# A static TensorE schedule: instruction blocks counted by true phase and size, and one output group split in two

## The chip, the cores and the metric

The program runs on one core of a Trainium2 chip. The metric is the device time in microseconds of one launch; of the kernel before there are three runs and one execution under the profiler. Engines are named as in the profile: PE (matmul; PEld is its weight load), DVE, ACT, POOL and SP (which only issues DMAs here).

## What is computed

A linear-attention recurrence over 768 steps (4 x 8 heads, state 40 x 40), whose output feeds two dense layers over 3072 tokens of width 320:

```
y[t]  = r[t] . state
Sa    = state . a[t]
state = state * w[t] - Sa (x) b[t] + v[t] (x) k[t]
x1 = gelu_like(x0 @ w_in) @ w_out            # d_ff 2048, h * sigmoid(1.702 h)
out = (silu(x1 @ w_gate) * (x1 @ w_val)) @ w_out2   # d_ff 1536
```

All inputs are float32. The small products of the recurrence are float32 matmuls; the wide ones split each operand into two float32r parts.

## The kernel before

**Three stages.** The recurrence is done in 12 steps of 64 tokens. Each step is some twenty small groups of matmuls (`Attention.prepare` builds a step's triangular inverse, `Attention.advance` its output and the next state), joined by work on DVE and ACT. The first dense layer (`Up`) needs the output of two steps for each of its six token blocks; its *wide parts* are 16 `h_part` (8 matmuls of 512 columns, L479) and 16 `o_part` (8 matmuls, L506 to L513) for each block, 192 in all. Recurrence and first layer are interleaved on PE by a planner; this is the stage up to some 739 us. The second layer (`Down`, L1392 and L1411 to L1413) follows, in an order of its own that the change does not touch. While the last wide parts run (the *tail* of the plan, after the last step's output), each `h_part` also sets off eleven small jobs that load and split `Down`'s weights.

**The planner.** `Plan.add` takes a task with its engine, a guessed cost, what it reads and writes, and a due time (for a step's groups its number, for wide parts 1e6: whenever nothing else is due). `Plan.order` simulates all engines and puts the tasks into one order, which the program then follows engine by engine without any choice at run time. So costs and rules of the planner set nothing but order, and how many *fillers* PE gets: `warm` (L437) is a matmul on zeros into a bank that nobody reads, put where PE would idle and its clock could fall.

**Instruction blocks in the planner.** The planner assumes that PE's instructions come in blocks of `BLOCK` = 256, and that a block takes `FETCH` = 3.8 us to come. `count` guesses a task's instructions from its cost, `cross` adds a stall where a task ends a block before the next is there, and two rules act on it: if a small group would run into a block's end too early, a wide part is taken first (`PACE`, `AHEAD`), and if none is ready, fillers bridge the gap (`BRIDGE`). A float32 matmul as written is two weight loads and two matmuls, so that a group of 32 is 128 instructions; a wide part is 16, a filler 2.

```
        c = t.choice["PE"]
        return 16 if t.due >= 1e6 or c < 1.05 else 128 if c < 1.7 else 256 if c < 3 else 384
```

The guess starts the count at 0 and takes 256 for the state update `m_one` of steps 1 to 4, which is 34 matmuls of two kinds and a drain.

**The output group.** In `advance`, `y_one` (L1115) multiplies the old state with r (`y_state` twice with a drain between, L1096) and then adds the part of the own tokens (`y_part`, L1110): one task of 64 matmuls on PE, cost 2.5. `y_mm` adds the last part, `y_out` on DVE scales the sum, `give` hands it to the dense layer.

**Accumulators of the first layer.** At the end of a token block the three accumulators in `sums` are drained by ACT L529, DVE L532, ACT L539 and DVE L541; the next block's first `o_part` (L511) waits for L541.

Of the kernel before, what the change touches and what calls it, by code (L numbers as in the profile page):

```python
# [51 lines left out]
class Task:  # L52
    def __init__(self, n, eng, cost, fn, deps, due, bank, kb, same, port):
        self.n, self.fn, self.due, self.deps, self.bank, self.kb, self.same = n, fn, due, deps, bank, kb, same
        self.port = port
        self.choice = dict(zip(eng, cost)) if isinstance(eng, tuple) else {eng: cost}
        self.pick = isinstance(eng, tuple)
        self.heirs, self.left, self.est = [], len(deps), {}
        self.eng = self.begin = self.end = None
# [12 lines left out]
class Plan:  # L72
# [4 lines left out]
    WINDOW, KEEP, DENSITY, WIDE, STILL = 3.4, 4000.0, 1600.0, 5000.0, 640.0  # L77
    BLOCK, FETCH, PACE, AHEAD = 256, 3.8, 0.5, 0.5
    BRIDGE = True
# [7 lines left out]

    def add(self, eng, cost, fn, reads=(), writes=(), due=0.0, after=(), bank=None, kb=0, into=(), same=None, port=True, work=None):
        deps = {d for d in after if d}
# [9 lines left out]
        t = Task(len(self.tasks), eng, cost, fn, deps, due, bank, kb, same, port)  # L99
        t.work = work  # L100
        for d in deps:
# [10 lines left out]
    def count(self, t):  # L112

        c = t.choice["PE"]
        return 16 if t.due >= 1e6 or c < 1.05 else 128 if c < 1.7 else 256 if c < 3 else 384

# [6 lines left out]
    def order(self):  # L123

        free, ready, done = {"PE": self.START}, {}, []
        sets = [0.0] * self.sets
        wire = port = hold = began = 0.0
        sent, pe = 0, []

# [23 lines left out]

        def cross(k, now, cost):
            nonlocal sent, began
            stop, left = 0.0, self.BLOCK - sent % self.BLOCK
            if k >= left:
                x = now + cost * left / k
                stop = max(0.0, began + self.FETCH - x)
                began = x + stop  # L160
            sent += k
            return stop

        def filler(t, now):
            w = self.fill(t, now)
            w.end += cross(2, now, w.end - now)
            done.append(w)
            pe.append((w.begin, w.end, self.STILL))
            return w.end
# [4 lines left out]
        while True:  # L174
# [8 lines left out]
            if e == "PE":  # L183
                k, size = self.count(t), self.BLOCK
                if t.due < 1e6 and (sent % size + k) / size * self.FETCH > now + t.choice[e] - began + self.PACE:
                    wide = [x for x in found if x[1] == 1e6 and x[0] <= now + self.AHEAD]
                    if wide:
                        now, _, _, e, t = wide[0]
                        k = self.count(t)
            for o in t.choice:  # L190
                ready[o].remove(t)
            if e == "PE":
# [4 lines left out]
                if t.due < 1e6 and hold < 1e8:  # L197
# [8 lines left out]
                    if self.BRIDGE:  # L206
                        left = size - sent % size
                        if k >= left:
                            x = began + self.FETCH - now - t.choice[e] * left / k
                            for _ in range(int(x / self.JUNK)):  # L210
                                now = filler(t, now)
                stop = cross(k, now, t.choice[e])
                pe.append((now, now + t.choice[e] + stop, load))
# [343 lines left out]
class Attention:  # L557
# [79 lines left out]
    def prepare(self, plan, n, due):  # L637
# [89 lines left out]

        plan.add("PE", 2.4, nb_mm, (ak, "kb1"), ("nb.p",), due + 0.15, bank=b, into=(nbk,), work=1760)
        plan.add(("ACT",), (1.05,), nb_out, ("nb.p",), (nbk,), due + 0.16, bank=b)
# [40 lines left out]
        def pieces():  # L770
# [89 lines left out]

            plan.add("PE", 2.7, cross_mm, ("xa", "dd"), ("x.p",), due + 0.1, bank=bx, into=("q0", "q1"), work=2900)
            plan.add(("ACT",), (0.62,), lambda e: move(e, bx, self.q), ("x.p",), ("q0", "q1"), due + 0.1, bank=bx)
            plan.add("PE", 2.3, join_mm, ("tn", "q0", "q1"), ("tt.p",), due + 0.1, bank=bt, into=("tt0", "tt1"), work=1280)
            plan.add(("ACT",), (0.62,), lambda e: move(e, bt, tt[:, :, 32:64]), ("tt.p",), ("tt0", "tt1"), due + 0.1,
# [87 lines left out]
    def advance(self, plan, n, due):  # L952
# [33 lines left out]
        if n:  # L986
            seen = plan.add("PE", 1.2, w_two, (ak, "mt"), ("w.p",), due, bank=bw)
        plan.add(("ACT",), (0.74,), w_out, ("w.p",), ("w",), due, bank=bw)
# [81 lines left out]
        if n + 1 < NT:  # L1070
            plan.add("PE", 2.6 if 0 < n < self.EARLY else 1.25, m_one, ("v", "tok0", "mt"), ("m.p",), due + 0.005, bank=bm,
                     work=4300 if 0 < n < self.EARLY else 2200, after=(middle,))
            plan.add("PE", 1.25, m_two, ("u", "tok1"), ("m.p",), due + 0.02, bank=bm, work=2200)
# [27 lines left out]
        def y_part(j, x):  # L1101
            ps = self.ps[by.slot]
            l = self.tok[j].rearrange("q i e -> q (i e)")
            for k in range(8):
                for r in range(2):
                    for p in range(2):
# [6 lines left out]
                        )  # L1113

        def y_one():  # L1115
            if n:
                y_state(1)
                nc.tensor.drain()
                y_state(0)
            y_part(0, self.sv)  # L1120
# [4 lines left out]
        def y_out():  # L1125
# [3 lines left out]

        plan.add("PE", 2.5 if n else 1.25, y_one, ("md", "r", "tok0", "sv"), ("y.p",), due + 0.045, bank=by,  # L1130
                 work=4300 if n else 2500, after=(marks,))
        plan.add("PE", 1.25, y_mm, ("tok1", "su"), ("y.p",), due + 0.05, bank=by, into=("su",),
# [645 lines left out]
```

## Time and profile before

| | us |
|---|---|
| median of 3 runs | 1143.59 |
| lowest and highest | 1138.55, 1144.63 |
| the profiled execution | 1140.57 |
| its span, first to last instruction | 1138.8 |
| PE busy | 1094.7 (96%) |
| DVE busy | 698.1 (61%) |
| ACT busy | 438.1 (38%) |
| POOL busy | 108.8 (10%) |

The span is the stretch that the profiler sees; the profiled execution's own time is 1.8 us longer. A matmul's end is modelled, so that "busy" hides short gaps between matmuls; idle time before an instruction is told apart by what ended it, and "issue" is a wait that ended with no semaphore: PE's sequencer had nothing to hand over.

### The profile page before, as it was taken

The numbers are of one execution on the slowest core, as the hardware profiler recorded it, in microseconds if no ns is written. First come the engines' busy times: TensorE is split into PE (matmuls) and PEld (weight loads), VectorE is DVE, ScalarE is ACT, GpSimd is POOL, SyncE is SP. The second block draws the span as 40 slices with busy tenths as digits, with TensorE's granted clock in tenths as the row PEclk, the third lists the DMA queues.
The fourth block names the chain that finished last, engine by engine and source line by source line (L and its number), as shares of the span: only waits on it lengthen the run. The fifth ranks groups of instructions, "written<-read, shape, count | busy, mean of one in ns | idle before, by whom it ended". The sixth has DMA issues, their size and how long they took to land.

```text
span 1138.8 us, 39991 instructions
## 1 busy us (share of the span) xinstructions
PE 1094.7 (96%) x17403; PEld 908.4 (80%) x17403; DVE 698.1 (61%) x1461; ACT 438.1 (38%) x809; POOL 108.8 (10%) x124
## 2 busy tenths in 40 slices
PE   9888999989999899999999989999999999999987
PEld 7667777767788777877788768788888888888877
DVE  7875788855968687787966166676344344434321
ACT  2434466543434343434335355545222222222221
POOL 1111223301010000000000022221000000000000
PEclk9898999999999999999899999999999999999999
DMA  7245457552534343443423265744233434343000
GB/s 217 88 154 166 149 165 226 159 177 73 180 103 151 112 137 117 134 150 91 145 64 112 83 204 161 218 122 111 75 106 99 129 103 144 93 127 91 24 1 27
DMA packets 141018, 141.99 MB, mean 125 GB/s; under 512 B 16032, under 2 KB 131744, under 8 KB 140832
## 3 DMA queue, kind: packets, MB, share of 16 engines
q1 hardware_dynamic: 134784, 131.48, 38.6%
q10 hardware_dynamic: 6048, 7.86, 2.1%
q8 instruction: 138, 2.26, 0.8%
q14 instruction: 48, 0.39, 0.1%
HBM read 118.04 MB, written 13.11 MB: 115 GB/s over the span
## 4 chain that ended last, share of the span: by engine, by line
PE 84%; DVE 6%; issue 3%; DMA 3%; SPq 2%; ACT 1%; POOL 0%; ACTq 0%; DVEq 0%; POOLq 0%
PE gv L1392 23%; PE h L479 13%; PE sums L511 4%; PE h L437 4%; PE oacc L1413 4%; PE oacc L1412 4%; PE oacc L1411 4%; PE sums L512 3%; PE sums L513 3%; PE ps L1110 2%; PE ps L1034 2%; PE ps L1160 2%; PE sums L507 2%; PE sums L506 2%; PE ps L885 1%
## 5 line engine op out<-in xcount | busy, mean ns | idle before, releaser
L1392 PE MATMUL gv<-xst,wg 128*128 128x512 f32 x1152 | 274.7, 391 | 0.0
L1392 PEld LDWEIGHTS gv<-xst,wg 128*128 128x128 f32 x1152 | 213.8, 188 | 41.3
L479 PE MATMUL h<-xst,wi 120*128 120x512 f32 x768 | 201.8, 405 | 0.4 <-ACT sg L487 0.3
L479 PEld LDWEIGHTS h<-xst,wi 120*128 120x128 f32 x768 | 142.0, 191 | 33.4 <-ACT sg L487 1.6
L1397 DVE TENSOR_TENSOR sg<-gv,sg 128x512 f32<-128x512 f32 x72 | 49.8, 691 | 169.9 <-PE gv L1392 169.2
L487 ACT ACTIVATE sg<-h 128x512 f32<-128x512 f32 x96 | 57.2, 596 | 174.7 <-PE h L479 162.9
L494 DVE TENSOR_TENSOR gl<-sg,gh 128x512 fp32r<-128x512 f32 x82 | 57.5, 701 | 81.7 <-ACT gh L493 81.7
L1398 ACT ACTIVATE gh<-sg 128x512 fp32r<-128x512 f32 x72 | 45.5, 632 | 137.1 <-DVE sg L1397 137.1
L307 POOL TENSOR_TENSOR cvw<-cvu,cva 128x256 uint32<-128x256 uint32 (+2 forms) x89 | 70.9, 798 | 251.1 <-DVE cvu L299 117.9
L1396 ACT ACTIVATE sg<-gv 128x512 f32<-128x512 f32 x72 | 42.9, 596 | 129.1 <-PE gv L1392 128.4
L1413 PE MATMUL oacc<-wo,gl 128*128 128x320 f32 x288 | 89.6, 311 | 0.0
L1412 PE MATMUL oacc<-wo,gh 128*128 128x320 f32 x288 | 89.4, 310 | 0.0
L1411 PE MATMUL oacc<-wo,gh 128*128 128x320 f32 x288 | 89.2, 310 | 0.0
L511 PE MATMUL sums<-gh,wo 128*128 128x512 f32 x192 | 82.0, 427 | 5.8 <-DVE sg L541 4.6
L1399 DVE TENSOR_TENSOR gl<-sg,gh 128x512 fp32r<-128x512 f32 x72 | 49.8, 692 | 50.3 <-ACT gh L1398 50.3
L512 PE MATMUL sums<-gh,wo 128*128 128x512 f32 x192 | 76.5, 399 | 0.0
L513 PE MATMUL sums<-gl,wo 128*128 128x512 f32 x192 | 76.1, 396 | 0.0
L437 PE MATMUL h<-still 128*128 128x512 f32 x232 | 71.4, 456 | 2.0 <-DVE still L396 1.2
L752 DVE TENSOR_TENSOR tsol<-tsol,tmp 128x126 f32<-128x126 f32 (+22 forms) x217 | 58.3, 269 | 6.7
L493 ACT ACTIVATE gh<-sg 128x512 fp32r<-128x512 f32 x96 | 60.7, 632 | 3.5
L744 DVE TENSOR_TENSOR tmp<-tsol,nsol 128x126 f32<-128x126 f32 (+22 forms) x217 | 56.9, 262 | 6.7
L437 PEld LDWEIGHTS h<-still 128*128 128x128 f32 x232 | 47.8, 217 | 12.9 <-DVE still L396 1.2
(176 smaller groups left out, 1652.9 us busy)
## 6 DMA issues: line engine op xcount, KB each, us to landing
wo<-w_out SPq DMA_DIRECT2D x192, 160.0 KB
cva<-out SPq DMA_DIRECT2D x128, 128.0 KB
cva<-gv SPq DMA_DIRECT2D x96, 128.0 KB
kb<-kba SPq DMA_DIRECT2D x92, 104.0 KB
cva<-in_ab SPq DMA_DIRECT2D x64, 120.0 KB
r<-rT SPq DMA_DIRECT2D x48, 104.0 KB
vt<-vT SPq DMA_DIRECT2D x48, 104.0 KB
a<-kba SPq DMA_DIRECT2D x46, 104.0 KB
```

The costliest lines, as they stand in the source:

```text
L307: nc.gpsimd.tensor_tensor(w.bitcast(U32), u, lo, op=ALU.add)
L437: self.nc.tensor.matmul(self.ph[0].rearrange("q (k c) -> q k c", k=4), c, c.unsqueeze(1).to_broadcast([128, 4, 128]), start=True, stop=True)
L479: nc.tensor.matmul(ps[:, 0:n], self.wi[:, b, 128 * f:128 * f + 128], x[:, a], start=(e == 0), stop=(e == 7))
L493: add("ACT", 0.63, lambda: nc.scalar.activation(out=hi, in_=sg, func=ACTF.Copy), (f"sg{s}",), (f"gh{d}",))
L511: nc.tensor.matmul(acc[k], w[:, c:c + 128], hi, start=st, stop=False)
L512: nc.tensor.matmul(acc[k], w[:, 256 + c:384 + c], hi, start=False, stop=False)
L513: nc.tensor.matmul(acc[k], w[:, c:c + 128], lo, start=False, stop=sp)
L752: self.engine(e).tensor_tensor(t, t, self.tmp[:, 0:(16 - o) * u].rearrange("q (c i) -> q c i", c=16 - o), op=ALU.add)
L1392: nc.tensor.matmul(ps, w[:, b], x[:, a], start=(i == 0), stop=(i == 7))
L1411: nc.tensor.matmul(acc[k], hi[:, c], self.wo[:, f, 0], start=st, stop=False)
L1412: nc.tensor.matmul(acc[k], hi[:, c], self.wo[:, f, 1], start=False, stop=False)
L1413: nc.tensor.matmul(acc[k], lo[:, c], self.wo[:, f, 0], start=False, stop=sp)
```

## The change

Four things change in the planner and in how tasks are declared to it. The count of instructions starts at 63 instead of 0 (`HEAD`), and tasks may give their true `size`. Each task gets a second duration, `least` (`real`), which is what the trace shows of it when nothing stops it, beside its guessed cost; the time that PE has worked in the block (`lean`) is added up from these. A block is now taken to need `FETCH` = 3.4 us, against a mean (`SURE` = 0.5) of that work and the planned time since the block began; `cross` may pass several block ends in one task. And `y_one` is cut in two tasks, `y_old` with both `y_state` (129 instructions) and `y_one` with `y_part`, between which other work may stand. No arithmetic is changed.

```
-    BLOCK, FETCH, PACE, AHEAD = 256, 3.8, 0.5, 0.5
+    BLOCK, FETCH, PACE, AHEAD, HEAD, SURE = 256, 3.4, 0.5, 0.5, 63, 0.5
...
     def count(self, t):
-        c = t.choice["PE"]
-        return 16 if t.due >= 1e6 or c < 1.05 else 128 if c < 1.7 else 256 if c < 3 else 384
+        return t.size or (16 if t.due >= 1e6 or t.choice["PE"] < 1.05 else 128)
+
+    def least(self, t):
+        c = t.choice["PE"]
+        return t.real or (1.87 if t.due >= 1e6 else min(c, 1.15))
...
-        sent, pe = 0, []
+        sent, pe = self.HEAD, []
...
-        def cross(k, now, cost):
-            nonlocal sent, began
-            stop, left = 0.0, self.BLOCK - sent % self.BLOCK
-            if k >= left:
-                x = now + cost * left / k
-                stop = max(0.0, began + self.FETCH - x)
-                began = x + stop
-            sent += k
+        def spare(x, y):
+            return began + self.FETCH - x if self.SURE >= 1.0 else self.FETCH - y - self.SURE * max(0.0, x - began - y)
+
+        def cross(k, now, cost, real):
+            nonlocal sent, began, lean
+            stop, part = 0.0, k
+            left = self.BLOCK - sent % self.BLOCK
+            while part >= left:
+                x = now + stop + cost * (k - part + left) / k
+                y = lean + real * left / k
+                stay = max(0.0, spare(x, y))
+                stop += stay
+                began, lean = x + stay, 0.0
+                sent, part, left = sent + left, part - left, self.BLOCK
+            sent += part
+            lean += real * part / k
             return stop
...
-                if t.due < 1e6 and (sent % size + k) / size * self.FETCH > now + t.choice[e] - began + self.PACE:
+                if t.due < 1e6 and (sent % size + k) / size * self.FETCH - self.PACE > self.FETCH - spare(
+                    now + t.choice[e], lean + self.least(t)
+                ):
...
-            plan.add("PE", 2.6 if 0 < n < self.EARLY else 1.25, m_one, ("v", "tok0", "mt"), ("m.p",), due + 0.005, bank=bm,
-                     work=4300 if 0 < n < self.EARLY else 2200, after=(middle,))
+            plan.add("PE", 2.6 if 0 < n < self.EARLY else 1.25, m_one, ("v", "tok0", "mt"), ("m.p",), due + 0.005, bank=bm,
+                     work=4300 if 0 < n < self.EARLY else 2200, after=(middle,),
+                     size=137 if 0 < n < self.EARLY else 128, real=2.5 if 0 < n < self.EARLY else 1.1)
...
+        def y_old():
+            y_state(1)
+            nc.tensor.drain()
+            y_state(0)
+
         def y_one():
-            if n:
-                y_state(1)
-                nc.tensor.drain()
-                y_state(0)
             y_part(0, self.sv)
...
-        plan.add("PE", 2.5 if n else 1.25, y_one, ("md", "r", "tok0", "sv"), ("y.p",), due + 0.045, bank=by,
-                 work=4300 if n else 2500, after=(marks,))
+        if n:
+            plan.add("PE", 1.25, y_old, ("md", "r"), ("y.p",), due + 0.045, bank=by, work=2200, after=(marks,), size=129)
+        plan.add("PE", 1.25, y_one, ("tok0", "sv"), ("y.p",), due + 0.045, bank=by, work=2100, after=(marks,))
```

Other tasks get `size=` or `real=` in the same way: `nb_mm` 256 and 1.44, `cross_mm` 261 and 2.5, `join_mm` 256 and 1.28, `w_two` 129.

In the built program PE has 220 fillers instead of 232; 48 instead of 40 wide parts stand in the tail. Line numbers of the change are 16 to 22 higher.

**First place: PE, the output of step 6** (L1160, in the change L1182, makes the scores; L1096, now L1116, is `y_state`; L1110, now L1130, is `y_part`; L479, now L495, is an `h_part`). Before:

```order
L1160 MATMUL ps_122<-r,ut 64x64 x32
L1096 MATMUL ps_123<-r,md 64x64 x2
L1096 MATMUL ps_123<-r,md 40x64 x2
...
L1110 MATMUL ps_123<-sv,tok_136 64x64 x2
L1110 MATMUL ps_123<-sv,tok_136 40x64 x2
...
L479 MATMUL h<-xst_93,wi 128x512 x8
```

and in the change:

```order
L1116 MATMUL ps_123<-r,md 64x64 x2
L1116 MATMUL ps_123<-r,md 40x64 x2
...
L495 MATMUL h<-xst_94,wi 128x512 x8
L1130 MATMUL ps_123<-sv,tok_136 64x64 x2
L1130 MATMUL ps_123<-sv,tok_136 40x64 x2
```

An `h_part` now stands between the two halves of the group; before, 96 small matmuls as written followed each other without a wide part.

**Second place: PE, the inverse of step 3** (L842 and L848, now L859 and L865, are `cross_mm`; L941, now L960, are the two token transposes; L511 is the first row of an `o_part`; L856, now L873, is `join_mm`). Before:

```order
L479 MATMUL h<-xst_93,wi 128x512 x8
L842 MATMUL ps_123<-cst 128x512
L848 MATMUL ps_123<-nsol,tsol 16x32 x64
L941 MATMUL ps_122<-cst,kb 128x104 x8
L511 MATMUL sums<-gh_99,wo_106 128x512
...
L856 MATMUL ps_123<-q,tn 32x32 x64
L437 MATMUL h<-still 128x512 x3
L941 MATMUL ps_122<-cst,kb 128x104 x8
L1160 MATMUL ps_123<-r,vt 64x64 x32
```

and in the change:

```order
L495 MATMUL h<-xst_93,wi 128x512 x8
L859 MATMUL ps_122<-cst 128x512
L865 MATMUL ps_123<-nsol,tsol 16x32 x64
L960 MATMUL ps_123<-cst,kb 128x104 x8
L960 MATMUL ps_122<-cst,kb 128x104 x8
L527 MATMUL sums<-gh_100,wo_105 128x512
...
L873 MATMUL ps_122<-q,tn 32x32 x64
L495 MATMUL h<-xst_93,wi 128x512 x8
L1182 MATMUL ps_122<-r,vt 64x64 x32
```

The second transpose moved ahead of the `o_part`, and an `h_part` stands in place of the three fillers behind `join_mm`.

**Third place: ACT, the accumulators of the fifth token block, in the tail** (L291, now L307, begins the work on a loaded weight piece `cva`; L1305, now L1327, rounds one; L529, now L545, drains the first accumulator). Before:

```order
L493 ACTIVATE gh_99<-sg_96 128x512
L291 ACTIVATE cva_76<-cva_76 128x256
L1305 ACTIVATE wo_10893<-cvw_79 128x256
L291 ACTIVATE cva_77<-cva_77 128x256
L529 ACTIVATE sg_98<-sums 128x512
```

and in the change:

```order
L509 ACTIVATE gh_99<-sg_96 128x512
L307 ACTIVATE cva_76<-cva_76 128x256
L1327 ACTIVATE wg<-cvw_79 64x2x128 x2
L545 ACTIVATE sg_98<-sums 128x512
```

One weight piece fewer stands between the rounding of `gh` and the first accumulator, since the tail's jobs begin four `h_part` earlier.

## Rows read from the trace of the kernel before

**Rows 1.** Page, head and part 1: span, busy time by engine.

```profile
span 1138.8 us, 39991 instructions
PE 1094.7 (96%) x17403; PEld 908.4 (80%) x17403; DVE 698.1 (61%) x1461; ACT 438.1 (38%) x809; POOL 108.8 (10%) x124
```

**Rows 2.** Windows by stage: length, busy of each engine (instructions), PE clock, DMA.

```profile
121.00:644.00 523.00, 503.69 (x12146) 405.82 (x12137) 380.36 (x821) 227.50 (x399) 54.40 (x51) 0.98 0.44 134
644.00:739.00 95.00, 90.59 (x379) 72.48 (x380) 57.94 (x126) 51.93 (x115) 23.32 (x30) 0.96 0.65 191
739.00:1138.80 399.80, 390.71 (x2016) 343.53 (x2014) 167.61 (x320) 113.44 (x208) 11.94 (x16) 0.99 0.30 89
```

**Rows 3.** Waits of PE: line, what it waited for, total, times, longest.

```profile
PE sums L511 <- DVE sg L541: 4.6, 2, 4.0
PE ps L941 <- issue: 4.5, 2, 3.0
...
PE ps L1096 <- DVE su L1166: 0.5, 1, 0.5
...
PE ps L996 <- issue: 0.2, 1, 0.2
```

**Rows 4.** DMA queues: the one that carries instructions (packets, MB, share).

```profile
q8 instruction: 138, 2.26, 0.8%
```

**Rows 5.** Timeline of PE, output of step 6: start, length, shape, count [idle before].

```profile
379.83 1.18 PE L1160 MATMUL ps<-r,ut 40*64 40x64 f32 x64
380.81 1.45 PE L1096 MATMUL ps<-r,md 40*64 40x64 f32 x64
382.07 0.53 PE L1110 MATMUL ps<-sv,tok 64*40 64x64 f32 x19
384.99 0.87 PE L1110 MATMUL ps<-sv,tok 64*64 64x64 f32 x45 [2.40 <-issue]
385.79 3.58 PE L479 MATMUL h<-xst,wi 120*128 120x512 f32 x8
```

**Rows 6.** Timeline of PE, the inverse of step 3.

```profile
181.06 0.39 PE L511 MATMUL sums<-gh,wo 128*128 128x512 f32 x1
...
182.08 1.25 PE L856 MATMUL ps<-q,tn 32*32 32x32 f32 x124
184.22 0.25 PE L856 MATMUL ps<-q,tn 32*32 32x32 f32 x4 [0.89 <-issue]
```

**Rows 7.** Timeline of PE, `nb_mm` of step 8 and the wait behind it.

```profile
431.49 1.44 PE L720 MATMUL ps<-kb,a 40*32 40x32 f32 x128
434.10 0.40 PE L511 MATMUL sums<-gh,wo 128*128 128x512 f32 x1 [1.17 <-issue]
```

**Rows 8.** Timeline of PE in step 9: small groups and an `o_part` without a wait.

```profile
522.95 1.14 PE L996 MATMUL ps<-w,tt 64*64 64x40 f32 x64
523.90 1.11 PE L1034 MATMUL ps<-v,tok 64*64 64x40 f32 x64
524.95 0.50 PE L511 MATMUL sums<-gh,wo 128*128 128x512 f32 x1
...
526.99 1.06 PE L1034 MATMUL ps<-u,tok 64*64 64x40 f32 x61
```

**Rows 9.** Timeline of PE: 43 fillers in a row.

```profile
20.75 10.04 PE L437 MATMUL h<-still 128*128 128x512 f32 x43
```

**Rows 10.** Chain that ended last, tail, fifth block's accumulators: start, us, what.

```profile
668.11 1.85 PE h L479 x8
...
674.49 3.75 DMA cva<-gv
...
678.66 0.58 ACT sg L529
...
681.36 0.80 PE sums L511
```

**Rows 11.** Windows: as rows 2, two stretches behind a wait.

```profile
386.00:389.50 3.50, 3.50 (x16) 2.27 (x19) 0.77 (x4) 0.09 (x1) 0.00 (x0) 0.51 0.16 53
679.60:686.40 6.80, 5.04 (x12) 3.98 (x13) 3.03 (x7) 2.87 (x6) 1.18 (x2) 0.50 0.74 241
```

**Rows 12.** Timeline of PE, step 10: a small group that waited for DVE.

```profile
562.68 1.34 PE L885 MATMUL ps<-tt,nb 32*32 32x32 f32 x64 [1.46 <-DVE nk L927]
563.95 1.95 PE L965 MATMUL ps<-v,nk 64*64 64x40 f32 x64
```

More of the change, by code (lines that the diff above doesn't have):

```diff
@@ L55, in __init__ @@
         self.port = port
+        self.work = self.size = self.real = None
         self.choice = dict(zip(eng, cost)) if isinstance(eng, tuple) else {eng: cost}
@@ L86, in __init__, with add @@
         self.sets = sets
-    def add(self, eng, cost, fn, reads=(), writes=(), due=0.0, after=(), bank=None, kb=0, into=(), same=None, port=True, work=None):
+    def add(self, eng, cost, fn, reads=(), writes=(), due=0.0, after=(), bank=None, kb=0, into=(), same=None, port=True, work=None,
+            size=None, real=None):
         deps = {d for d in after if d}
@@ L99, in add @@
         t = Task(len(self.tasks), eng, cost, fn, deps, due, bank, kb, same, port)
-        t.work = work
+        t.work, t.size, t.real = work, size, real
         for d in deps:
@@ L126, in order @@
         sets = [0.0] * self.sets
-        wire = port = hold = began = 0.0
-        sent, pe = 0, []
+        wire = port = hold = began = lean = 0.0
+        sent, pe = self.HEAD, []
         def offer(t):
@@ L165, in filler @@
             w = self.fill(t, now)
-            w.end += cross(2, now, w.end - now)
+            w.end += cross(2, now, w.end - now, 0.23)
             done.append(w)
@@ L208, in order @@
                         if k >= left:
-                            x = began + self.FETCH - now - t.choice[e] * left / k
+                            x = spare(now + t.choice[e] * left / k, lean + self.least(t) * left / k)
                             for _ in range(int(x / self.JUNK)):
                                 now = filler(t, now)
-                stop = cross(k, now, t.choice[e])
+                stop = cross(k, now, t.choice[e], self.least(t))
                 pe.append((now, now + t.choice[e] + stop, load))
@@ L726, in nb_out @@
             self.copy(e, self.flat(nb), self.ps[b.slot].rearrange("q r x -> q (r x)"), -1.0)
-        plan.add("PE", 2.4, nb_mm, (ak, "kb1"), ("nb.p",), due + 0.15, bank=b, into=(nbk,), work=1760)
+        plan.add("PE", 2.4, nb_mm, (ak, "kb1"), ("nb.p",), due + 0.15, bank=b, into=(nbk,), work=1760,
+                 size=256, real=1.44)
         plan.add(("ACT",), (1.05,), nb_out, ("nb.p",), (nbk,), due + 0.16, bank=b)
@@ L859, in move @@
                 self.copy(e, dst, self.ps[b.slot][:, 0].rearrange("q (i t) -> q i t", t=32))
-            plan.add("PE", 2.7, cross_mm, ("xa", "dd"), ("x.p",), due + 0.1, bank=bx, into=("q0", "q1"), work=2900)
+            plan.add("PE", 2.7, cross_mm, ("xa", "dd"), ("x.p",), due + 0.1, bank=bx, into=("q0", "q1"), work=2900,
+                     size=261, real=2.5)
             plan.add(("ACT",), (0.62,), lambda e: move(e, bx, self.q), ("x.p",), ("q0", "q1"), due + 0.1, bank=bx)
-            plan.add("PE", 2.3, join_mm, ("tn", "q0", "q1"), ("tt.p",), due + 0.1, bank=bt, into=("tt0", "tt1"), work=1280)
+            plan.add("PE", 2.3, join_mm, ("tn", "q0", "q1"), ("tt.p",), due + 0.1, bank=bt, into=("tt0", "tt1"), work=1280,
+                     size=256, real=1.28)
             plan.add(("ACT",), (0.62,), lambda e: move(e, bt, tt[:, :, 32:64]), ("tt.p",), ("tt0", "tt1"), due + 0.1,
@@ L986, in advance @@
         if n:
-            seen = plan.add("PE", 1.2, w_two, (ak, "mt"), ("w.p",), due, bank=bw)
+            seen = plan.add("PE", 1.2, w_two, (ak, "mt"), ("w.p",), due, bank=bw, size=129)
         plan.add(("ACT",), (0.74,), w_out, ("w.p",), ("w",), due, bank=bw)
```

## Prediction

> **What bounds the kernel now.** I read the page's head first: PE is busy in 96% of the span [rows 1], so only what stands on PE itself can shorten it. Next the windows by stage: the second layer, 739 to 1138.8 us, keeps PE busy in 391 of 400 us [rows 2], and the change does not touch it. What the change can move lies in the first 739 us, above all in the steps from 121 to 644 us, where PE is busy 504 of 523 us at a mean clock of 0.98, and in the tail behind them [rows 2].
>
> Then the waits of PE. Eleven of its rows end with "issue", from 4.5 us down to 0.2 us, and sum to 18.6 us [rows 3]; no semaphore ended them. The timeline shows what they are. In the output of step 6 PE stops for 2.40 us in the midst of one group, after 19 of its 64 matmuls [rows 5]; in `join_mm` of step 3 it stops 0.89 us after 124 of 128 [rows 6]. Nothing inside a group waits for another engine. Counting PE's instructions in the built program (two weight loads and two matmuls for each float32 matmul as written, drains and semaphore waits too), these two stops stand within two places of 72 x 256 + 193 and 35 x 256 + 193, and the one behind `nb_mm` [rows 7] of 80 x 256 + 193. So they recur by blocks of 256. The queue of kind "instruction" carried 138 packets of 16.4 KB each [rows 4], while PE ran 34,806 matmuls and weight loads [rows 1], 252 for each packet. I take it from this that PE stops where the next block of 256 has not come, and that the block ends lie at 193 behind a multiple of 256, that is, 63 places off a count from 0. From one block end to the next such a stop took 3.2 us (181.06 to 184.22, [rows 6]) and about 4.8 us (from 380.2, inside the group of L1160, to 384.99, [rows 5]).
>
> The Trainium skill, in "Runtime: NRT & Kernel Launch", section "Instruction fetch mechanics", says of such blocks that "The cost of crossing a 16 KiB boundary is one DMA tail-bump, mostly hidden". The blocks agree; "mostly hidden" does not agree with 2.40 us of idle PE inside a group [rows 5]. By that rule the fetch would cost nothing, and only the fillers of the sum below would be left; it is the second rival.
>
> **The change, part by part.**
>
> *Blocks counted right.* What counts is how much work a block holds. From rows without a wait: a group of 32 matmuls as written takes 0.95 to 1.05 us from start to start, an `o_part` before a small group 2.04 us [rows 8], a wide part before another 1.85 us [rows 10], `y_state` 1.26 us [rows 5], a filler 10.04/43 = 0.23 us [rows 9]. A block with two small groups holds about 2.1 to 2.3 us and stops PE for a microsecond or more; one with a wide part in it holds 3.4 to 4.1 us and does not. I laid such durations under both orders and cut them at the 117 true block ends of the recurrence. Before, 17 blocks hold under 3.0 us, after the change 9, and behind the third step 8 and 2. If a block needs 3.4 us, the shortfalls sum to 18.4 us before, which is what the issue waits sum to (18.6, [rows 3]), and to 10.3 us after: **-8.1 us**. At 3.2 us it is -7.9, at 4.0 us -8.5, at 4.8 us -4.4, at 3.0 us -6.7. So the gain hardly hangs on the block's time. Bounds: nothing, if PE's own work was the late one, and -18.6 if all goes. The stops of rows 5, 6 and 7 are among those that go; what is left stands in the first two steps, whose order hardly changes, where DVE is late next.
>
> *The output group in two.* The two halves hold the same matmuls and one drain, so nothing is added but the change from wide to small: an `h_part` between them makes the next small group begin 2.04 instead of 1.85 us later, 0.2 us. Over the whole order such changes go from 104 to 105: **+0.2 us**. What the cut gives is in the block sum.
>
> *Fillers.* 12 fewer, each 0.23 us: **-2.8 us**; nothing of it where they stood in a wait for DVE. I take it whole, since PE has wide parts to put there, and the tail takes up what is left.
>
> *New waits.* Small groups stand closer in the early steps of the changed order, and PE meets the engines that serve it sooner. The trace has such waits at 0.5 us (L1096 for DVE, [rows 3]) up to 1.46 us [rows 12]. I take six at 0.5 us, the nearer row, since from step 2 on a wide part can stand before each: **+3.0 us**; the ends are 0 and six at 1.46, +8.8.
>
> *The tail.* There L511 waits 4.0 us for the last accumulator [rows 3]. The chain says why: a weight piece `cva<-gv` took from 674.49 to 678.24 us to come, ACT and DVE stood at it, and only then drained the accumulators, 678.66 to 681.36, 2.7 us [rows 10]. The clock then stood at 0.50 for 6.8 us, in which PE's 5.04 us of work would have been half [rows 11]: 6.5 us lost in all. In the changed order the piece that ACT takes before L529's place stands on SP's queue a whole wide part earlier, ahead of a set of `wo` loads, and not behind copies `wg<-wg` that wait for DVE; so it should be there. What is late next: DVE has two subtractions ahead of the first accumulator, some 0.8 us, and the 2.7 us of draining, against an `h_part` of 1.85 us; PE then waits 1.5 us and the clock stays. **-5.0 us**; the ends are -6.5 and 0.
>
> *The clock elsewhere.* The stop of rows 5 was followed by 3.5 us at 0.51 [rows 11], in which an `h_part` took 3.58 us instead of some 2.0 [rows 5]. That goes with the stop, 1.5 us; each new wait can bring as much. I count 0, with ends at -1.5 and +3.
>
> Sum: -8.1 + 0.2 - 2.8 + 3.0 - 5.0 = -12.7 us. The profiled execution took 1140.57 us, so 1127.9 for one like it; the median of the three runs stands 3.0 us above it, which makes **1131 us**.
>
> **The rivals.**
>
> *The tail's wait stays.* The accumulators' wait is a matter of when one load comes, and a load can be late in the changed order too. Then the -5.0 is lost: 1136 us.
>
> *Not the fetch.* If the stops come from something that goes with PE's instruction count but is not met by more work in a block (the page's rule above, or fetches that come late under load, as 4.8 us does), the block sum gives nothing and the tail half: 1143.6 + 0.2 - 2.8 + 3.0 - 2.5 = 1141.5 us. For it: the stops differ from 0.89 to 2.40 us at like blocks. Against: the shortfalls give the sum of the waits without a free number but 3.4.
>
> *The change counts badly too.* The planner does not count the waits on semaphores that the built program puts on PE; by the tail its count is 70 places behind the true one, a quarter of a block. My block sum has the true places in it, so this is paid already, but a late block falls in the steps where the count is worst. If only the steps to the sixth gain, about half of the 8.1 goes: 1135 us.
>
> *DVE takes over, and it is slower.* Place: `q_mm` and the groups behind the inverse of steps 5 to 11, which wait for DVE's masks and its chain of small products; DVE is busy 380 of 523 us there [rows 2]. Each such wait costs 1.46 us, and the clock falls behind it: the next group took 1.95 us [rows 12] where a like one takes 1.14 [rows 8]. If that lasts as long as behind the tail's wait, it costs 2.5 us [rows 11], so 4.0 us each. If five of the seven steps have it anew, 20 us come on top of the forecast: 1151 us. It decides from four on, where it eats up the gain. Against it: one such wait of this size stands in the whole trace of those steps, and the changed order keeps about as many wide parts for each of them.
>
> **How the numbers follow.** The measurement of this kernel can tell about 0.5% (5.7 us) from no change, so "faster" is below 1137.9 and "slower" above 1149.3. Forecast 1131 with its own range of 1121 to 1138: 0.55. Tail stays, 1136: 0.10. Half the blocks, 1135: 0.06. These three are faster: 0.71. Not the fetch, 1141.5: 0.20, the same. DVE takes over: 0.09, slower. The lower end of the range is the forecast with no new waits, all of the tail and two more stops gone (-3.0 - 1.5 - 1.5 - 2.4, about -9): 1122. The upper end takes in the second rival at 1142; beyond lie DVE's case and the ends of the others, some 2 in 10.
>
> **What would show it.** Issue waits of PE near 10 us instead of 18.6; no stop inside `y_part` of step 6 nor in `join_mm` of step 3; stops, where left, again at 193 behind a multiple of 256; 220 fillers; L511's wait for L541 near 1.5 us; the recurrence over some 15 us or more before 644, with eight more wide parts behind it. It would be wrong if the issue waits fell and waits for DVE rose by as much, if they did not fall at all, or if the clock stood at 0.5 in more stretches than before.

## The result, and the profile after

| | before | change |
|---|---|---|
| median (lowest to highest; runs) | 1143.83 us (1138.55 to 1145.18; 6) | 1129.42 us (1118.69 to 1133.10; 6) |
| the profiled execution | 1140.57 | 1129.72 |
| its span | 1138.8 | 1127.9 |
| first matmul of the second layer | 734.88 | 725.23 |

The ratio is 0.9868 (95% interval 0.9819 to 0.9917). A second comparison gave 1124.82 against 1138.79, 0.9879 (0.9835 to 0.9923). So the change is 1.3% faster, some 14 us. Here and below medians are of all executions, and ratios leave out those more than 1.5% above the fastest of their kernel (one execution of the kernel that tests the tail took 1490.62 us).

Page of the change, head and part 1, and its windows by stage (columns as in [rows 1, 2]):

```profile
span 1127.9 us, 39970 instructions
PE 1084.3 (96%) x17391; PEld 899.3 (80%) x17391; DVE 701.9 (62%) x1468; ACT 437.8 (39%) x809; POOL 103.9 (9%) x117
```

```profile
121.00:644.00 523.00, 506.07 (x12024) 406.70 (x12023) 388.16 (x847) 231.13 (x410) 50.78 (x45) 0.98 0.45 136
644.00:727.00 83.00, 80.30 (x341) 64.94 (x341) 56.15 (x123) 49.83 (x110) 22.41 (x31) 0.98 0.72 212
727.00:1127.90 400.90, 391.51 (x2026) 344.11 (x2025) 161.53 (x303) 109.94 (x198) 9.25 (x12) 1.00 0.29 85
```

PE is the bound as before. Of the 10.9 us by which the span is shorter, 9.7 are gained ahead of the second layer, whose order is unchanged. The waits of PE in the change (line, what it waited for, total, times, longest), some of the largest, and those that answer to [rows 3]:

```profile
PE ps L865 <- issue: 3.4, 1, 3.4
...
PE ps L960 <- issue: 2.5, 2, 1.6
PE ps L960 <- ACT q L643: 2.5, 1, 2.5
PE sums L527 <- DVE sg L557: 2.1, 1, 2.1
PE ps L736 <- issue: 2.0, 4, 0.9
PE ps L913 <- issue: 1.9, 1, 1.9
...
PE ps L904 <- DVE nk L946: 0.8, 1, 0.8
```

The rows with "issue" sum to 16.4 us (before 18.6, [rows 3]); the prediction said near 10. The accumulators' wait in the tail, 4.0 us before, is 2.1. Now the places that the prediction named. Timeline of PE, output of step 6 in the change (first its `y_state`, then `y_part`), and `join_mm` of step 3:

```profile
367.99 1.49 PE L1116 MATMUL ps<-r,md 40*64 40x64 f32 x64
369.40 2.11 PE L495 MATMUL h<-xst,wi 120*128 120x512 f32 x8
371.44 1.15 PE L1130 MATMUL ps<-sv,tok 64*64 64x64 f32 x64
372.38 1.14 PE L1130 MATMUL ps<-su,tok 64*40 64x64 f32 x64
```

```profile
178.32 0.48 PE L527 MATMUL sums<-gh,wo 128*128 128x512 f32 x1
...
180.35 1.20 PE L873 MATMUL ps<-q,tn 32*32 32x32 f32 x119
182.42 0.27 PE L873 MATMUL ps<-q,tn 32*32 32x32 f32 x9 [0.87 <-issue]
```

The stop of 2.40 us inside the output [rows 5] is gone: a wide part lies between the halves and the clock stays. The stop in `join_mm` [rows 6] is still there, nearly as long, though that block had 4.1 us from its start: by count of PE's instructions it began with the `o_part` at 178.32, and the next one began at 182.42.

The recurrence ends 21 us earlier; its last output group before, and in the change:

```profile
642.84 1.15 PE L1110 MATMUL ps<-su,tok 64*64 64x64 f32 x64
```

```profile
621.69 1.15 PE L1130 MATMUL ps<-su,tok 64*64 64x64 f32 x64
```

### The profile page after: what moved, and what is told of

The parts are those of the page before. It is cut to its first block, busy times and chain, and to the rows that moved or that the text cites. A ratio compares the mean times of both kernels' runs of the same rounds, so it can differ in the third digit from the quotient of the medians.

```text
span 1127.9 us, 39970 instructions
## 1 busy us (share of the span) xinstructions
PE 1084.3 (96%) x17391; PEld 899.3 (80%) x17391; DVE 701.9 (62%) x1468; ACT 437.8 (39%) x809; POOL 103.9 (9%) x117
## 5 line engine op out<-in xcount | busy, mean ns | idle before, releaser
L495 PE MATMUL h<-xst,wi 120*128 120x512 f32 x768 | 203.5, 408 | 0.6 <-ACT sg L503 0.6
L495 PEld LDWEIGHTS h<-xst,wi 120*128 120x128 f32 x768 | 144.0, 193 | 33.9 <-ACT sg L503 1.1
L510 DVE TENSOR_TENSOR gl<-sg,gh 128x512 fp32r<-128x512 f32 x87 | 60.5, 696 | 64.7 <-ACT gh L509 64.4
L323 POOL TENSOR_TENSOR cvw<-cvu,cva 128x256 uint32<-128x256 uint32 (+2 forms) x89 | 73.6, 828 | 250.9 <-DVE cvu L315 82.6
L1421 DVE TENSOR_TENSOR gl<-sg,gh 128x512 fp32r<-128x512 f32 x72 | 49.9, 693 | 50.3 <-ACT gh L1420 50.3
L529 PE MATMUL sums<-gl,wo 128*128 128x512 f32 x192 | 75.7, 394 | 0.0
L453 PE MATMUL h<-still 128*128 128x512 f32 x220 | 65.1, 440 | 1.3 <-DVE still L412 1.2
L1433 PEld LDWEIGHTS oacc<-wo,gh 128*128 128x128 f32 x288 | 54.1, 188 | 2.7
```

The costliest lines, as they stand in the source:

```text
L323: nc.gpsimd.tensor_tensor(w.bitcast(U32), u, lo, op=ALU.add)
L453: self.nc.tensor.matmul(self.ph[0].rearrange("q (k c) -> q k c", k=4), c, c.unsqueeze(1).to_broadcast([128, 4, 128]), start=True, stop=True)
L495: nc.tensor.matmul(ps[:, 0:n], self.wi[:, b, 128 * f:128 * f + 128], x[:, a], start=(e == 0), stop=(e == 7))
L510: add(("DVE", "POOL"), (0.74, 1.35), lambda e: self.engine(e).tensor_tensor(lo, sg, hi.bitcast(F32), op=ALU.subtract), (f"sg{s}", f"gh{d}" ...
L529: nc.tensor.matmul(acc[k], w[:, c:c + 128], lo, start=False, stop=sp)
L1433: nc.tensor.matmul(acc[k], hi[:, c], self.wo[:, f, 0], start=st, stop=False)
```

## The experiments

All are read against the kernel before on the same chip. "Shortfall" is what the expectations call the sum of what the blocks lack of 3.4 us.

### Parts of the change

**The cut alone**: the kernel before with `y_one` in two tasks, nothing else.

```
...
+        if n:
+            plan.add("PE", 1.25, y_old, ("md", "r"), ("y.p",), due + 0.045, bank=by, work=2200, after=(marks,))
+        plan.add("PE", 1.25, y_one, ("tok0", "sv"), ("y.p",), due + 0.045, bank=by, work=2100, after=(marks,))
```

> The kernel before with nothing but the output group cut in two (y_old, y_one). Its order has 221 fillers, 40 wide parts in the tail as before, and block shortfalls at 3.4 us of 20.2 us (18.4 before, 10.3 in the change). Theory 1, the block count gives the gain: no gain here, 1140 to 1146 us, issue waits 18 to 21 us. Theory 2, the cut gives it, since a wide part can stand inside the group: 1130 to 1136 us.

**The phase alone**: the kernel before with the count from 63 and the true size of the early `m_one`.

```
-        return 16 if t.due >= 1e6 or c < 1.05 else 128 if c < 1.7 else 256 if c < 3 else 384
+        return 137 if c == 2.6 else 16 if t.due >= 1e6 or c < 1.05 else 128 if c < 1.7 else 256 if c < 3 else 384
...
-        sent, pe = 0, []
+        sent, pe = 63, []
```

> The kernel before with nothing but the count started at 63 and m_one of steps 1 to 4 counted as 137; FETCH 3.8, the old rules and the whole output group stay. 216 fillers, 48 wide parts in the tail, block shortfalls at 3.4 us 12.4 us against 18.4 before. Theory 1: half or more of the gain, 1130 to 1137 us, issue waits 12 to 15 us. Theory 2, the rules on traced durations or the cut are what gives it: 1140 to 1146 us.

**Half a block off**: the change with a wrong phase.

```
-    BLOCK, FETCH, PACE, AHEAD, HEAD, SURE = 256, 3.4, 0.5, 0.5, 63, 0.5
+    BLOCK, FETCH, PACE, AHEAD, HEAD, SURE = 256, 3.4, 0.5, 0.5, 191, 0.5
```

> The change with the count started at 191 instead of 63, half a block off; all else as in the change (226 fillers, 48 wide parts in the tail). Block shortfalls at 3.4 us: 23.0 us against 10.3. Theory 1, the true phase matters: some 10 to 13 us slower than the change, 1139 to 1143 us, issue waits 22 us or more. Theory 2, the gain is the tail's and the clock's and any such order has it: within 4 us of the change, 1126 to 1133 us.

**The change without the cut.**

```
...
+        plan.add("PE", 2.5 if n else 1.25, y_one, ("md", "r", "tok0", "sv"), ("y.p",), due + 0.045, bank=by,
+                 work=4300 if n else 2500, after=(marks,), size=257 if n else 128, real=2.3 if n else 1.15)
```

> The change with the output group left in one task (true size 257). Laid under the true block ends, its shortfalls at 3.4 us sum to 16.2 us (before 18.4, the change 10.3), with 231 fillers (before 232) and 59 wide parts in the tail. Theory 1 (the block shortfalls carry the gain): 2 us less than before, 1140 to 1142 us, issue waits of PE 16 to 17 us. Theory 2 (true phase and sizes carry it whatever the shortfalls, by fewer stretches at half clock): 1128 to 1133 us, mean clock 0.984 or more. If the cut alone carries it: 1142 to 1146 us, clock 0.979 or less.

**Phase and cut, old rules**: the two first edits together, `FETCH` 3.8, no second duration.

> The kernel before with the count started at 63, 137 for m_one of steps 1 to 4, and the output group cut in two; the old rules and 3.8 us stay. Shortfalls at 3.4 us: 11.8 us, 220 fillers, 40 wide parts in the tail. Each of the two parts alone gave about 13 us. If the two gains add up: 1114 to 1119 us. Theory 1 (both only move block ends; time follows the shortfalls): 1128 to 1132 us, issue waits near 12 us. If the new rules (two durations, 3.4 us) are a part of the gain by themselves: 1133 us or more.

| | median | ratio to before (95%) | issue waits | other waits, 33 to 760 us |
|---|---|---|---|---|
| cut alone | 1127.32 | 0.9872 (0.9801 to 0.9943) | 19.4 | 10.0 |
| phase alone | 1129.31 | 0.9902 (0.9864 to 0.9940) | 16.2 | 11.4 |
| phase and cut, old rules | 1134.28 | 0.9872 (0.9825 to 0.9918) | 14.2 | 15.9 |
| the change | 1129.42 | 0.9868 (0.9819 to 0.9917) | 16.4 | 11.9 |
| half a block off | 1147.03 | 1.0084 (1.0041 to 1.0127) | 20.9 | 12.1 |
| without the cut | 1153.66 | 1.0091 (1.0053 to 1.0129) | 19.6 | 24.3 |

(The cut's one profile was of its longest execution, 1138.84 us. The rows come from several chips, so that ratios are to be compared, not medians; half a block off and phase alone ran on one chip.) Four orders come out alike, at about 0.99: parts that bring 1% or more alone do not add up. The cut alone is as fast as the change, and its profile shows issue waits as long as before (18.6 to 19.9 us in three profiles, below): theory 1, no gain without shorter waits, failed there. What the cut gains by itself is not shown; the median clock of its five executions is 0.985, of the kernel before 0.979.

The change's rules with the phase half a block off lose all of the gain, with the longest issue waits of all. So the new rules as such bring nothing; with them, the true phase decides. Only one wrong phase was run; that part of this is the chance of one order is not excluded. How much of that is stops and how much clock, the windows of two of these kernels say. From 121 to 644 us, half a block off and then phase alone (the figure before the last two is PE's granted clock):

```profile
121.00:644.00 523.00, 502.25 (x12083) 404.03 (x12082) 379.67 (x827) 222.06 (x393) 52.96 (x46) 0.96 0.44 132
```

```profile
121.00:644.00 523.00, 505.71 (x12160) 406.08 (x12161) 392.29 (x849) 231.36 (x415) 56.09 (x52) 1.00 0.46 139
```

The issue waits moved less than expected (16.2 us for 12 to 15, 20.9 for 22 or more), the times more. The issue waits differ by 4.7 us, the medians by 17.7 us. The rest goes with the clock, 0.96 in one and 1.00 in the other.

Without the cut the kernel is slower than before, and not by the issue waits alone: small groups stand closer, 59 wide parts are left for the tail, and PE waits longer for ACT and DVE, 14.6 us from 121 to 645 us (before 4.8) and 7.0 from there to 760 (before 4.3). Waits of PE of that kernel:

```profile
PE sums L527 <- DVE sg L557: 6.1, 4, 2.0
PE h L495 <- ACT sg L503: 5.7, 6, 2.4
...
PE ps L960 <- ACT md L643: 3.7, 1, 3.7
```

The simplest reading of theory 1 fell with it too: shortfall 16.2 (before 18.4) was to give 1140 to 1142.

### Does a block really take 3.4 us?

**A stream on one place.** Ahead of the first `w_one` of the change, 384 small matmuls on zeros, then six times 60 with 8 fillers. It adds work on zeros and leaves nothing out.

```
...
+        def small(k):
+            for _ in range(k):
+                self.nc.tensor.matmul(out[0:64, 0:64], c[0:64, 0:64], c[0:64, 64:128], start=True, stop=True)
+
+        small(384)
+        for _ in range(6):
+            small(60)
+            for _ in range(8):
+                self.warm()
...
```

> The change with a stream put before the first w_one: 1536 PE instructions of small float32 matmuls on zeros (384 as written, 64x64) without any wait, then six blocks of 60 such matmuls and 8 fillers. It adds work and leaves none out. Blocks of 256 that must be fetched: the first half stops once per 256 instructions at 193 behind a multiple of 256, from stop to stop 3.2 to 3.6 us, so some 20 us for 12.5 us of matmuls; the second half, 3.9 us of work per block, does not stop. If fetching is hidden: no stop in either half, the first takes 12.5 us.

It took 1220.56 us and missed its question. All went to one place of the array, and there 1488 matmuls took 88.0 us, 59 ns each:

```profile
L462 PE MATMUL h<-still 64*64 64x64 f32 x1488 | 88.0, 218 | 0.0
```

A block of 256 then held 7.6 us of work, and no block could be late.

**The stream round four quadrants and two banks.**

```
+        c, out = self.still.bitcast(F32), (self.ph[0], self.acc[2])
...
+            for i in range(k):
+                e, t, o = 64 * (i // 2 % 2), 64 * (i % 2), 64 * (i // 4 % 8)
+                self.nc.tensor.matmul(
+                    out[e // 64][t:t + 64, o:o + 64], c[e:e + 64, 0:64], c[e:e + 64, 64:128], start=True, stop=True
+                )
...
```

> The change with a stream on PE ahead of the first step's w_one: 384 small float32 matmuls as written, 64 x 64 on zeros, that go round the four quadrants of the array and two banks (1536 instructions, six blocks), then six times 60 of them and 8 fillers (256 instructions each time). A group of 32 small ones took 1.0 us elsewhere, so a block of them alone holds some 2.1 us of work, one with fillers 3.8 us. Theory 1 (a block needs about 3.4 us to come): five or six stops in the first part, 256 instructions apart, from start to start 3.2 to 3.6 us, each 1.1 to 1.5 us, 6 to 9 us in all; no stop in the second part. Rival (blocks come late only under other load, or the stops come from something else): no stop in the first part, which then takes 13 us, or stops at other distances.

1168.38 us; theory 1 held. The issue waits in the stream, and the six matmuls behind a stop (timeline; start, length, idle before):

```profile
PE sums L463 <- issue: 8.5, 6, 1.6
```

```profile
35.85 0.27 PE L463 MATMUL sums<-still 64*64 64x64 f32 x1 [0.90 <-issue]
39.58 0.27 PE L463 MATMUL sums<-still 64*64 64x64 f32 x1 [1.64 <-issue]
43.03 0.27 PE L463 MATMUL sums<-still 64*64 64x64 f32 x1 [1.36 <-issue]
46.76 0.27 PE L463 MATMUL sums<-still 64*64 64x64 f32 x1 [1.64 <-issue]
50.49 0.27 PE L463 MATMUL sums<-still 64*64 64x64 f32 x1 [1.64 <-issue]
53.94 0.27 PE L463 MATMUL sums<-still 64*64 64x64 f32 x1 [1.36 <-issue]
```

They lie 3.73, 3.45, 3.73, 3.73 and 3.45 us apart, and the second part, whose blocks hold more work, has none. The queue that carries instructions moved one packet for each of them (packets, MB, share, from 31.2 to 54.3 us):

```profile
q8 instruction: 6, 0.10, 1.8%
```

In the trace these packets start at 33.47, 37.02, 40.77, 44.06, 47.79 and 51.58 us and take 0.93 to 1.33 us each. PE went on 1.21 to 1.56 us after each had landed, and the next started 1.03 to 1.19 us after that. It is so in the kernels too: the fourteen traces of this case hold 268 issue waits of over 0.15 us, and all but one end 1.18 to 1.66 us after a packet of that queue has landed and stand at place 193 or 194 behind a multiple of 256 among PE's recorded instructions. So the issue waits are waits for the next block. In the stream a block took about 3.6 us at a DMA share of 0.19; in step 3 one took 4.1 (above). Windows of both parts:

```profile
31.20:54.30 23.10, 14.56 (x890) 13.64 (x889) 11.97 (x21) 0.91 (x2) 1.47 (x2) 1.00 0.19 54
54.30:90.00 35.70, 34.53 (x1125) 27.54 (x1125) 3.78 (x9) 6.28 (x12) 2.44 (x3) 1.00 0.05 15
```

PE stood idle for 8.5 of 23.1 us, and yet its clock was 1.00.

### The tail

**The kernel before, the jobs behind the drain.** Both batches of eleven jobs ahead of the fifth block's accumulator drain go behind it; PE's order stays.

```
...
                         if hasattr(t, "last"):
-                            down.prepare(11)
+                            owed += 11
+                        if owed and (left < 20 or not any(getattr(x, "sums", False) for x in tail[i + 1:i + 9])):
+                            down.prepare(owed)
+                            owed = 0
```

> The kernel before, with the two batches of eleven small jobs that stand ahead of the fifth token block's accumulator drain put behind it; PE's order is untouched. The prediction's tail term: L511's wait of 4.0 us falls to 0 to 1.5 us, the 6.8 us at half clock behind it go, and the kernel gains 5 us: 1136 to 1139 us. Rival: the wait is worth less than that, since the lost clock comes back at another place or the later jobs make the second layer wait: 1140 to 1144 us.

1141.32 us against 1144.46, 0.9964 (0.9926 to 1.0002). Its timeline at the accumulators, and the tail's window:

```profile
687.85 0.50 PE L511 MATMUL sums<-gh,wo 128*128 128x512 f32 x1 [0.92 <-DVE sg L541]
```

```profile
644.00:740.00 96.00, 93.37 (x635) 74.32 (x634) 58.18 (x121) 52.51 (x113) 23.50 (x29) 1.00 0.62 184
```

The wait fell from 4.0 to 0.92 us and the tail's clock from 644 us on is 1.00 (before 0.96, [rows 2]). The gain, 3 to 4 us, is smaller than the 5 predicted, and its interval reaches from 8 us to nothing.

### What a stop costs with its clock

**Stops put into the second layer.** The change, with the lag of that layer emptied four times in each block; no work is added or left out.

```
-                if len(self.lag) > self.LAG:
+                while len(self.lag) > (0 if f in (2, 3, 6, 7) else self.LAG):
```

> The change with the second layer's lag emptied behind the third, fourth, seventh and eighth part of each of its six blocks, so that PE has to wait for the chain of ACT and DVE some 12 times; no work is added. In that layer the clock was 1.00 and PE never stopped, so this shows what a stop costs with its clock. Chain: one multiply 0.7, one copy 0.6 and one subtraction 0.7 us and three semaphores, 2.5 to 3 us a stop, 30 to 36 us in all. If the clock falls to half behind each such stop for 3.4 us, as behind the stop inside the output of step 6: 1.5 to 1.7 us more for each, 18 to 20 us, total 1177 to 1186 us, and the layer's mean clock near 0.94. Rival: the clock stays at 1.00, as it did through the six stops of 0.9 to 1.6 us of the stream of small matmuls: 1159 to 1166 us.

1159.94 us, at the rival's lower end. The waits are shorter than the chain led me to think; waits of PE and one of the thirteen places:

```profile
PE oacc L1433 <- ACT gh L1420: 20.3, 13, 2.1
...
PE oacc L1435 <- DVE gl L1421: 2.2, 13, 0.2
```

```profile
773.62 0.42 PE L1433 MATMUL oacc<-wo,gh 128*128 128x320 f32 x1 [1.51 <-ACT gh L1420]
```

The waits sum to 22.5 us; the layer took 35.4 us longer than in the change (first matmul at 719.98). Twelve of the thirteen were 1.51 us long. In the records of the granted clock, half speed for 3.4 us lies behind four of these twelve (at 749.3, 821.0, 960.9 and 1100.9 us) and behind none of the others. Four times 1.7 us and the waits make 29.3; where the other 6 us went, the trace doesn't say. So both expectations have a part: like stops cost the clock sometimes.

### Twice the same, and a try at a better one

**The change, and the kernel before, once more** (no edit).

> The change itself once more, for a second profile beside the run above on the same chip. 1125 to 1133 us. If the prediction's block term was right on average, issue waits of PE near 10 to 12 us this time; if the first profile was typical, 15 to 18 us.

> The kernel before once more, for a second profile. 1136 to 1147 us, issue waits 17 to 20 us, L511's wait near 4 us; if its stretches at half clock are a matter of the single execution and not of the order, most of them lie at other places than in the first profile.

The change took 1124.82 us, the kernel before 1146.97 in its one execution. With the tail's kernel (PE's order of before) and the second layer's stops (the change's order up to 720 us) there are three profiles of each order, in the order of before / again / tail, and change / again / stops:

| | before | change |
|---|---|---|
| issue waits, all | 18.6, 19.9, 19.6 | 16.4, 13.3, 15.0 |
| 0 to 121 us | 7.3, 8.8, 7.4 | 9.1, 7.6, 9.7 |
| 121 to 390 us | 9.6, 7.0, 7.3 | 6.5, 5.5, 4.6 |
| 390 to 645 us | 1.9, 4.2, 5.0 | 0.8, 0.3, 0.6 |
| other waits, 33 to 760 us, without the tail's accumulators | 6.9, 9.0, 10.7 | 9.8, 11.0, 10.4 |
| half clock before the second layer, us | 44.4, 47.8, 51.2 | 30.7, 37.6, 23.9 |

The half-clock stretches are no accident of one execution on the whole: the order of before had one near 440 or 386 us and one near 564 to 573 us each time, the changed order none from 390 to 645 us in any of the three.

What PE did before its clock fell is nearly always the same. In these six traces 42 half-clock stretches begin between 33 and 700 us, 41 of them within 2.5 us of the end of an idle stretch of PE of over 0.3 us. That stretch was an issue wait for 18 in the three profiles of before and for 11 in the three of the change; those hold 35 and 24 us at half clock per profile on average. The reverse does not hold: 144 such idle stretches end there, most of them with no fall behind them.

**A leaner rule and the tail's edit, on the change.**

```
-    BLOCK, FETCH, PACE, AHEAD, HEAD, SURE = 256, 3.4, 0.5, 0.5, 63, 0.5
+    BLOCK, FETCH, PACE, AHEAD, HEAD, SURE = 256, 3.4, 0.5, 0.5, 63, 0.25
...
+                        if owed and (left < 20 or not any(getattr(x, "sums", False) for x in tail[i + 1:i + 9])):
...
```

> The change with SURE 0.25 instead of 0.5, and the two batches of eleven small jobs put behind the fifth block's accumulator drain. Shortfalls at 3.4 us 8.4 us (the change 10.3), 216 fillers (220), 40 wide parts in the tail (48). If shortfalls, fillers and the tail's wait pay as they are counted: 2 + 1 + 2 us less than the change, about 1124 us, at the same clock. Rival: the order's small differences move waits and half-clock stretches by as much as that, so that it can't be told from the change: 1126 to 1134 us.

1125.85 us beside 1124.82 of the change: nothing gained. Its timeline of the tail shows where the tail's term went: PE at the accumulators and at the second `h_part` behind them, and ACT in between:

```profile
670.82 0.50 PE L527 MATMUL sums<-gh,wo 128*128 128x512 f32 x1 [0.92 <-DVE sg L557]
...
679.16 2.70 PE L495 MATMUL h<-xst,wi 120*128 120x512 f32 x8 [2.52 <-ACT sg L503]
```

```profile
676.47 0.44 ACT L307 ACTIVATE cva<-cva 128x256 uint32<-128x256 uint32 x1 [2.41 <-DMA cva<-gv]
```

The wait for the accumulators is 1.1 us shorter, but ACT now stands 2.41 us at a weight piece behind the drain, as it stood ahead of it before the change, and PE waits 2.52 us for ACT. The late load only moved. No version run here beats the change.

## Why the prediction was right, point by point

**The total.** 1131 was forecast and 1129.42 measured; the profiled execution lost 10.9 us against the 12.7 of the sum. That PE stops for late blocks of 256 is shown by the stream and by the packets of the instruction queue. The recurrence ended 21 us earlier, as forecast (15 or more). The terms came out otherwise; they are taken from the three profiles of each order.

- **Blocks, -8.1 forecast.** The issue waits fell by 4.5 us (means 19.4 and 14.9). This is a term that was mis-sized. Over the eight orders whose shortfall is on record the issue waits do follow it, from 13.3 us at a shortfall of 8.4 to 20.9 at 23.0, but by about 0.54 us for each us; the 18.4 that met 18.6 in the kernel before has no match in the orders with less shortfall. Behind 121 us they fell by 5.6, where the count had 8 short blocks before and 2 after; ahead of it, where I left the shortfall nearly as it was, they rose by 1.0, and a block that took 4.1 us and not 3.4 still stops PE in step 3. "No stop in `join_mm`" was wrong, "no stop in the output of step 6" right, "near 10 us" wrong. The stops that are left again stand at 193 or 194 behind a multiple of 256.
- **Fillers, -2.8.** There are 220 as said; nothing contradicts the term, and no run tests it alone.

```profile
L453 PE MATMUL h<-still 128*128 128x512 f32 x220 | 65.1, 440 | 1.3 <-DVE still L412 1.2
```

- **New waits, +3.0.** Other waits rose by 1.5 us (8.9 to 10.4), within the term's ends; the largest new one, L960 for ACT in step 3, took 2.5, 1.2 and 1.3 us. Without the cut they took 12 us more, so the forecast's worry was real for another order.
- **The tail, -5.0.** Its wait went from 4.0 us to between 2.0 and 2.1 instead of 1.5 (the forecast's own terms, 0.8 + 2.7 - 1.85, make 1.65): ACT found its weight piece, as forecast, and then waited 1.37 us for DVE's first drain, 0.6 more than before. The clock fell behind it in two of three profiles. So -2 for the wait is measured; the rest of the term hung on the clock.

```profile
671.58 0.59 ACT L555 ACTIVATE sg<-sums 64x512 f32<-64x512 f32 x1 [1.37 <-DVE sg L548]
```

- **The clock elsewhere, 0.** This is where the forecast was most off. Over the 39 executions of the kernel before that these ratios use (1131 to 1148 us) the time goes with the mean granted clock, with a correlation of -0.88 and 10.9 us for each 0.01. The medians are 0.980 there and 0.987 over 11 executions of the change, which is 8 us of the 14 between the pooled medians (1141.0 and 1126.9); at 0.985 on both lines 1134.2 and 1128.3 are left, 6 us. So about half of the gain goes with the clock. The prediction took the fall behind the stop of step 6 for one case of 1.5 us and left it out of the sum; of the 17 us at half clock that the change saves per profile, 11 stood behind issue waits. An 0.01 of the span is 23 us at half speed, so about half of a half-clock stretch is lost. The Trainium skill, in "TensorE: Matmul & The Clock Gate", section "Terms", counts that loss as the throttled time times one less the granted share, which is half; the 11 of 23 us agree.

So the total is right in part by luck, since errors met: issue waits gave some 4 us less than forecast and the tail's wait a little less, the clock some 6 us or more that the sum did not have. The terms of the forecast's lower end add to -8.4, not -9, which moves it by half a us.

**The rivals.** "Not the fetch" fell with the stream: 8.5 idle us in 23.1, all of it every 256 instructions, each time behind a packet of instructions. The Trainium skill ("Runtime: NRT & Kernel Launch", "Instruction fetch mechanics") calls the crossing "mostly hidden"; that holds for blocks that hold more work than their fetch takes, as in the stream's second part, and not for small matmuls. "Counts badly too" had the wrong place: from 390 to 645 us, late in the count, the issue waits fell from 3.7 to 0.6 us on average, and the first steps gave nothing. "The tail's wait stays" was half true. "DVE takes over" did not come: the group of step 10 that waited 1.46 us [rows 12] no longer waits, and the half clock behind it is gone; the 0.8 us for L946 stand in step 11. Step 10 in the change:

```profile
544.16 1.20 PE L904 MATMUL ps<-tt,nb 32*32 32x32 f32 x64
545.29 1.14 PE L984 MATMUL ps<-v,nk 64*64 64x40 f32 x64
```

**What stays open.** Why the clock falls behind some stops and not behind others of the same length; and why cut, phase and both give the same 1%, the cut without shorter issue waits. A floor set by the first two steps does not explain it: behind 121 us the cut's profile still has 13.4 us of issue waits, those of the change 5.2 to 7.3. Nor was it tried how far orders differ by chance, with other phases or small changes of the rules.

## What to carry to other kernels

Where an engine runs long stretches of short instructions, lay its program out in blocks of 256 and compare the work of each with the 3.2 to 4.8 us that late blocks took here. Check the phase of the count: half a block off cost 2.2% against the true one. Price a stop with the clock behind it, from runs of one kernel against its mean granted clock, before any difference of a per cent is put down to the waits that a profile lists. And take several profiles of each order: issue waits of one order differed by 3 us from one execution to the next.

## What the hardware showed beside that

- Small matmuls on one place of the array took 59 ns from one to the next; sent round four quadrants and two banks, four began every 0.06 us.
- PE stopped six times for 0.9 to 1.6 us within 23 us, and its granted clock stayed at 1.00; behind stops of 1.51 us between long wide matmuls it fell to half four times in twelve.
- Blocks in the stream came every 3.45 or 3.73 us, two values only. Of that some 1.1 us passed before the packet started, 0.9 to 1.3 us in its transfer, and 1.2 to 1.6 us from its landing until PE went on.
